# Attention and a mixture of experts in one kernel: weight splits from both ends of the table, norms ahead of the last score products, and sums of squares on TensorE

## The chip, the core and the metric

The kernel is one program on 1 core of a Trainium2 chip. The metric is device time in microseconds (us) of one execution, lower is better. The engines are named as in the profile: PE (TensorE matmul), PEld (TensorE weight load), DVE (VectorE), ACT (ScalarE), POOL (GpSimd) and SP (SyncE, which here only issues DMAs).

## What is computed

Attention over channels for four batches, then a mixture of experts with one expert per token:

```python
# q, k, v: 4 x 5056 x 256 (float32)
qn = q / (norm(q, axis=1) + 1e-06); kn = k / (norm(k, axis=1) + 1e-06)
a = softmax(kn.transpose(0, 2, 1) @ qn / tau)      # 4 x 256 x 256
x = (v @ a).reshape(20224, 256)
e = argmax(x @ w_gate, axis=1); g = softmax(x @ w_gate)[e]
out = g * (relu(x @ w1[e]) @ w2[e])                # 8 experts, 256 -> 1024 -> 256
```

## The kernel before, in words

**Attention** is the generator `attention(b, ...)` (L177). It walks over 20 chunks of 256 tokens of q and k. A chunk (tile `raw`, 128 x 1024 float32) is loaded by two DMAs (L190, L191), squared on ACT (L200, L202) and added into `ssq` on DVE (L203), and multiplied on PE into the score accumulators `sp` in PSUM. Batch 0 and chunks 1 to 13 of batch 1 multiply float32 as it is (L209, two instructions of 128x256 for each product, eight for a chunk). The other chunks are first split into a high and a low float32r part (L173 on ACT, L174 on DVE) and multiplied as such (L213, L214). Batch 1's chunk 0 is split as well, since its 512 wide products open both halves of the accumulators.

After the last chunk come the norms: `ssq` is folded (L220), summed over the partitions by four products with ones (L223, tile `ntp`), a row of 128x4 operations on DVE makes the reciprocal norms (L229 to L242), and the scores become the softmax `a_x` (L263 to L298).

Then ten groups g0 to g9 of 512 tokens follow: load of v (L308), `px` = v times `a_x` on PE (L322), four copies and four sums of squares on ACT (L327, L329), routing on DVE and PE (L335 to L399, with the products `rtp` L380, L383), scaled rows (L343, L344) and four scatters into a table in DRAM on POOL (L402). The loads of chunks and of v take turns in a ring of three tiles (`raw`), and SP issues its DMAs strictly in order.

**Weights** are the generator `weights()` (L92). Sixteen matrices of 1 MB, n = 0 to 15 (w1 and w2 of eight experts), are loaded as float32, each into the place in `W` of the next matrix (`raw = place(n + 1)`, L111; the last one into a tile of its own). PE sums their squares (`gram`, L137, 16 products), DVE takes the diagonal (`w_diag`, L140), PE adds it up (L144) and DVE makes the scales of an expert (`pow2`, L82, L83). Then a matrix is split: ACT writes the high halves and DVE the low ones, into place n.

```python
act.activation(hi, src, AF.Copy, scale=sw)                                   # L105
vec.scalar_tensor_tensor(out=lo, in0=src, scalar=sw, in1=hi, ...)            # L106
```

Split n writes over the raw values of matrix n - 1, so ACT can start split n only when DVE has finished split n - 1: one chain of 16 splits.

**What sets the order.** The program is written as a loop over steps (L658): after batch 0's chunks each step takes half a group of batch 0, two yields of `weights()` (one split) and one chunk of batch 1, ten chunks in all. `table(0)` (L457) comes after group g5 and makes the list of the first expert blocks from the counts so far. A scheduler then fixes the order of the instructions on each engine; each engine works strictly in that order. From the first block on (L548 to L610) expert blocks run to the end, with the rest of the attention in between.

Of the kernel before, what the change touches and what calls it, by code (L numbers as in the profile page):

```python
# [20 lines left out]
P = 128  # L21
B, N, C = 4, 5056, 256
NP = 5120
E, F = 8, 1024
# [6 lines left out]
CUT = 6  # L31
# [30 lines left out]
def attention_then_experts(ctx, tc, q, k, vT, tau, w_gate, w1, w2, kc, out):  # L62
    nc = tc.nc
    sync, act, vec, pool, pe = nc.sync, nc.scalar, nc.vector, nc.gpsimd, nc.tensor

    one = ctx.enter_context(tc.tile_pool(name="one", bufs=1))
    work = ctx.enter_context(tc.tile_pool(name="work", bufs=2))
    tiny = ctx.enter_context(tc.tile_pool(name="tiny", bufs=2))
    dram = ctx.enter_context(tc.tile_pool(name="dram", bufs=1, space=bass.MemoryType.DRAM))
    ps_a = ctx.enter_context(tc.tile_pool(name="ps_a", bufs=2, space=bass.MemoryType.PSUM))  # L70
    ps_h = ctx.enter_context(tc.tile_pool(name="ps_h", bufs=3, space=bass.MemoryType.PSUM))
    ps_y = ctx.enter_context(tc.tile_pool(name="ps_y", bufs=1, space=bass.MemoryType.PSUM))
# [17 lines left out]
    last_load = [None]  # L90

    def weights():  # L92

        def place(n):
            return W[:, n // 2, (n % 2) * 4096 : (n % 2 + 1) * 4096]

        scales = one.tile([P, E, 2], F32, name="scales")
        later = []
        ready = []

        def split_one():
            nonlocal ready
            if ready:
                hi, lo, src, sw = ready.pop(0)
                act.activation(hi, src, AF.Copy, scale=sw)  # L105
                vec.scalar_tensor_tensor(out=lo, in0=src, scalar=sw, in1=hi, op0=ALU.mult, op1=ALU.subtract)  # L106

        for n in range(2 * E):
            e, w = divmod(n, 2)
            if n < 2 * E - 1:  # L110
                raw = place(n + 1).bitcast(F32)  # L111
            else:
                raw = work.tile([P, 2048], F32, tag="hl", name="wraw", bufs=2)
            for h in range(2):
                with tc.issue_after(last_load[0]):
                    if w == 0:
                        sync.dma_start(
                            out=raw.rearrange("p (q d f) -> p q d f", q=4, d=2)[:, :, h, :],
                            in_=w1[e, h * P : (h + 1) * P, :].rearrange("p (q f) -> p q f", q=4),
                        )  # L120
                    else:
                        sync.dma_start(
                            out=raw[:, h * 1024 : (h + 1) * 1024].rearrange("p (f d) -> p f d", d=C),
                            in_=w2[e, h * 512 : (h + 1) * 512, :].rearrange("(f p) d -> p f d", p=P),
                        )
                if h == 0:
                    split_one()
                yield

            top = raw.bitcast(BF16)[:, 1::2]  # L130
            if w == 0:
                gram = ps_h.tile([P, 512], F32, tag="hp", name="gram")
                dsum = tiny.tile([P, 2], F32, name="w_dsum")
            own = gram[:, w * P : (w + 1) * P]
            for i in range(16):
                part = top[:, i * P : (i + 1) * P]
                pe.matmul(own, part, part, start=(i == 0), stop=(i == 15))  # L137
            diag = work.tile([P, P], F32, tag="o", name="w_diag", bufs=2)

            vec.scalar_tensor_tensor(  # L140
                out=diag, in0=own, scalar=1.02, in1=ident, op0=ALU.mult, op1=ALU.mult, accum_out=dsum[:, w : w + 1]
            )
            if w == 1:
                pe.matmul(gram[:, 2 * P : 2 * P + 2], ones, dsum, start=True, stop=True)  # L144
                pow2(scales[:, e, :], gram[:, 2 * P : 2 * P + 2], 10)
            sw = scales[:, e, w : w + 1]

            d4 = place(n).rearrange("p (k s x) -> p k s x", k=8, s=2)
            later.append((d4[:, :, 0, :], d4[:, :, 1, :], raw.rearrange("p (k x) -> p k x", k=8), sw))
            if w == 1:  # L150
                ready, later = ready + later, []
# [12 lines left out]
    NATIVE = 14  # L164
# [9 lines left out]
        vec.tensor_tensor(out=hl[:, 1], in0=raw, in1=hl[:, 0], op=ALU.subtract)  # L174
        return hl

    def attention(b, s_split, x_split, acc):  # L177

# [3 lines left out]
        sp = [pool_.tile([P, 2, C], F32, tag=tag, name=f"sp{c}") for c, (pool_, tag) in enumerate(acc)]  # L182
        ssq = one.tile([P, 2, 512], F32, tag="a_l", name="ssq")
        nch = len(s_split)
        for ch in range(nch):

            tag, bufs = (("raw", RAW), ("rows", 3), ("xg", 2), ("raw", RAW), ("rows", 3))[ch % 5 if b == 0 else 0]
            raw = work.tile([P, 2, 512], F32, tag=tag, name="raw", bufs=bufs)
            sl = slice(2 * ch, 2 * ch + 2)
            sync.dma_start(out=raw[:, :, 0:C], in_=qv[b][:, sl, :])  # L190
            load = sync.dma_start(out=raw[:, :, C:512], in_=kv[b][:, sl, :])  # L191
            if b == 0:
                last_load[0] = load.ins
            if s_split[ch]:
                hl = split(raw)
                sq = raw
            else:
                sq = work.tile([P, 2, 512], F32, tag="hl", name="sq", bufs=2)
            if ch == 0:
                act.activation(ssq, raw, AF.Square)  # L200
            else:
                act.activation(sq, raw, AF.Square)  # L202
                vec.tensor_tensor(out=ssq, in0=ssq, in1=sq, op=ALU.add)  # L203
            for j in range(2):
                first, last = ch == 0 and j == 0, ch == nch - 1 and j == 1
                for c in range(2):
                    kc0 = C + c * P
                    if not s_split[ch]:
                        pe.matmul(  # L209
                            sp[c][:, 0, :], raw[:, j, kc0 : kc0 + P], raw[:, j, 0:C], start=first, stop=last  # L210
                        )
                        continue
                    pe.matmul(sp[c], hl[:, 0, j, kc0 : kc0 + P], hl[:, :, j, 0:C], start=first, stop=False)  # L213
                    pe.matmul(  # L214
                        sp[c][:, 1, :], hl[:, 1, j, kc0 : kc0 + P], hl[:, 0, j, 0:C], start=False, stop=last
                    )
            yield 2 * 640


# [1 line left out]
        tp = ps_t.tile([P, 512], F32, tag="tp", name="ntp")  # L221
        for i in range(4):
            pe.matmul(tp[:, i : i + 1], ssq[:, 0, i * P : (i + 1) * P], ones[:, 0:1], start=True, stop=True)  # L223

        def four(name):
            return tiny.tile([P, 4], F32, name=name)

        ss, y, h = four("n_ss"), four("n_y"), four("n_h")
        vec.tensor_scalar(out=ss, in0=tp[:, 0:4], scalar1=1e-30, scalar2=None, op0=ALU.max)  # L229
# [383 lines left out]
    def run(gen):  # L613
        for _ in gen:
            pass
# [132 lines left out]
```

## Time and profile before

| | |
|---|---|
| runs | 1222.15, 1226.06, 1227.25 us, median 1226.06 |
| the profiled execution | 1222.09 us, span 1220.2 us, mean granted clock 0.988 of 2.4 GHz |
| PE busy | 1161.4 us (95% of the span) |
| DVE, ACT, POOL busy | 904.7 (74%), 645.3 (53%), 383.5 us (31%) |
| PE busy, tenths in the first 8 of 40 slices | 8 8 8 8 7 8 9 8, then 9 nearly throughout |
| DMA busy, the same slices | 9 9 8 9 6 8 5 4 |

A slice is 30.5 us. Busy shares are averages over stages with different limits, so the stages are read one by one below. PE is close to full after the first 150 us; what it leaves free lies ahead of that.

### The profile page before, as it was taken

What the parts mean: (1) busy time and instruction counts of PE and PEld (TensorE: products, weight loads), DVE (VectorE), ACT (ScalarE), POOL (GpSimd) and SP (SyncE); (2) the same over time, 40 slices, a digit from 0 to 9 for tenths busy, and PEclk for the clock granted to TensorE, in tenths of its full rate; (3) what the DMA queues carried; (4) which work ended last, traced back from release to release, by engine and by line L of the source; (5) the groups of instructions that cost most, each with busy time, mean ns of one, the idle gap of its engine ahead of it and who ended that gap; (6) DMA issues with size and microseconds to landing.
All of it is one profiled execution on the core that took longest, in us unless ns stands there. A gap on an engine that the chain in (4) does not pass through costs nothing. (4 is left out here: it accounts for less than half of the span.)

```text
span 1220.2 us, 28272 instructions
## 1 busy us (share of the span) xinstructions
PE 1161.4 (95%) x10212; PEld 1025.4 (84%) x10212; DVE 904.7 (74%) x2384; ACT 645.3 (53%) x1362; POOL 383.5 (31%) x366
## 2 busy tenths in 40 slices
PE   8888789988899999999999999999999999999998
PEld 7767578877788889888888888889888888888897
DVE  5689789677787777777788777777676656656886
ACT  5388864776655545666655545666523332332322
POOL 0027651444521122444441112444431111111111
PEclk9889999999999999999999999999999999999999
DMA  9989685444355433444354534433241222221221
GB/s 302 351 278 316 156 206 136 117 122 131 103 137 127 136 84 96 119 121 109 94 152 114 138 87 96 114 114 79 62 114 48 53 53 53 49 45 42 43 50 33
DMA packets 196830, 145.91 MB, mean 120 GB/s; under 512 B 117580, under 2 KB 176337, under 8 KB 196688
## 3 DMA queue, kind: packets, MB, share of 16 engines
q1 hardware_dynamic: 181296, 102.48, 34.2%
q0 software_dynamic: 15392, 41.60, 9.5%
q8 instruction: 81, 1.33, 0.5%
q14 instruction: 61, 0.50, 0.1%
HBM read 80.03 MB, written 43.29 MB: 101 GB/s over the span
## 5 line engine op out<-in xcount | busy, mean ns | idle before, releaser
L571 PE MATMUL hp<-xT,wp 128*128 128x256 f16 (+1 forms) x4320 | 452.1, 263 | 5.1 <-issue 1.4
L594 PE MATMUL y<-wp,ht 128*128 128x256 f16 x3888 | 450.3, 273 | 6.4 <-DVE ht L579 2.7
L594 PEld LDWEIGHTS <-ht 128*128 128x128 f16 x3888 | 372.4, 98 | 68.1 <-issue 10.4
L571 PEld LDWEIGHTS <-wp 128*128 128x128 f16 x4320 | 383.8, 98 | 52.1 <-issue 6.1
L605 POOL DMA_INDIRECT out<-o,mt x162 | 184.3, 1138 | 649.6 <-ACT o L603 612.4
L559 DVE COPY wp<-W 128x1024 f16 x720 | 297.6, 428 | 111.9 <-PE y L594 64.4
L578 ACT ACTIVATE ht<-hp 128x512 f16<-128x512 f32 x324 | 191.2, 595 | 201.3 <-PE hp L571 162.8
L579 DVE SCALAR_TENSOR_TENSOR ht<-hp,ht 128x512 f16<-128x512 f32 x324 | 220.4, 685 | 36.8 <-ACT ht L578 31.5
L402 POOL DMA_INDIRECT xs<-rows,r_si x160 | 182.3, 1139 | 145.8 <-ACT xjunk L329 50.1
L603 ACT ACTIVATE o<-y,b_fac 128x256 f32<-128x256 f32 x162 | 68.8, 469 | 175.5 <-PE y L594 161.3
L325 PE MATMUL px<-a_h,hl 128*128 128x264 f32 x480 | 99.1, 296 | 1.3 <-ACT xg L327 0.8
L343 ACT ACTIVATE rows<-xg,x_sc 128x256 f16<-128x256 f32 x160 | 69.2, 498 | 35.7 <-issue 16.3
L325 PEld LDWEIGHTS px<-a_h,hl 128*128 128x128 f32 x480 | 79.1, 188 | 4.1 <-issue 1.8
L174 DVE TENSOR_TENSOR hl<-raw,hl 128x1024 fp32r<-128x1024 f32 x47 | 57.4, 1221 | 30.7 <-ACT hl L173 30.7
L213 PE MATMUL sp<-hl 128*128 128x512 f32 x188 | 72.4, 418 | 1.0 <-DVE hl L174 1.0
L173 ACT CAST hl<-raw 128x1024 fp32r<-128x1024 f32 x47 | 49.1, 1044 | 45.0 <-PE sp L214 40.0
L209 PE MATMUL sp<-raw 128*128 128x256 f32 x264 | 64.0, 394 | 9.0 <-DMA raw<-in_k 9.0
L202 ACT ACTIVATE raw<-raw 128x1024 f32<-128x1024 f32 x44 | 46.6, 1058 | 44.6 <-DVE hl L174 42.5
L344 DVE SCALAR_TENSOR_TENSOR rows<-xg,x_sc,rows 128x256 f16<-128x256 f32 x160 | 69.1, 478 | 0.6 <-issue 0.2
L325 PE MATMUL px<-a_l,hl 128*128 128x264 f32 x240 | 68.6, 286 | 0.0
L329 ACT ACTIVATE xjunk<-xg 128x256 bf16<-128x256 f32 x160 | 66.7, 417 | 3.1
L327 ACT COPY xg<-px 128x264 f32<-128x264 f32 x160 | 57.8, 367 | 14.2 <-PE px L325 6.9
(140 smaller groups left out, 925.6 us busy)
## 6 DMA issues: line engine op xcount, KB each, us to landing
raw<-in_q SPq DMA_DIRECT2D x80, 256.0 KB
raw<-in_k SPq DMA_DIRECT2D x80, 256.0 KB
vraw<-in_vT SPq DMA_DIRECT2D x40, 512.0 KB
W<-in_w SPq DMA_DIRECT2D x30, 512.0 KB
out<-o,mt POOLq DMA_INDIRECT x162
xs<-rows,r_si POOLq DMA_INDIRECT x160
xT<-xs SPq DMA_TRANSPOSE x90
xs<-pad SPq DMA_DIRECT2D x9, 129.0 KB
```

The source lines that it names most:

```text
L213: pe.matmul(sp[c], hl[:, 0, j, kc0 : kc0 + P], hl[:, :, j, 0:C], start=first, stop=False)
L325: pe.matmul(px, hl[:, vh, c, ts], ah[:, c, :], start=(n == 0), stop=(n == 5))
L343: act.activation(r16[:, t, 0:C], x, AF.Copy, scale=sc[:, t : t + 1])
L344: vec.scalar_tensor_tensor(out=r16[:, t, C : 2 * C], in0=x, scalar=sc[:, t : t + 1], in1=r16[:, t, 0:C], op0=ALU.mult, op1=ALU.subtract,)
L402: ins = pool.indirect_dma_start(out=xs[:, :], out_offset=bass.IndirectOffsetOnAxis(ap=si[:n, t : t + 1], axis=0), in_=rows[:n, t, :], in_o ...
L559: vec.tensor_copy(out=t, in_=Wf[:, ds(e * 8192 + n * 1024, 1024)])
L571: pe.matmul(hp[:, f % nf, :], wp[:, dc, wh, (f % 2) * P : (f % 2 + 1) * P], xT[:, 2 * xh + dc, :], start=(n == 0), stop=(n == 5),)
L578: act.activation(ht[:, 0], hp, AF.Relu)
L579: vec.scalar_tensor_tensor(out=ht[:, 1], in0=hp, scalar=0.0, in1=ht[:, 0], op0=ALU.max, op1=ALU.subtract)
L594: pe.matmul(ys[j], hts[f // nf][:, hh, f % nf, j * P : (j + 1) * P], wp[:, f % 2, wh, :], start=(f == 0 and n == 0), stop=(f == 7 and n == 2),
L603: act.activation(o, ys[j], AF.Copy, scale=fac[:, j : j + 1])
L605: pool.indirect_dma_start(out=out[:, :], out_offset=bass.IndirectOffsetOnAxis(ap=mt.bitcast(I32)[:, j, 1:2], axis=0), in_=o, in_offset=Non ...
```

## The change

It has four parts. The lines are those of the changed kernel where they carry a +.

1. `weights()` takes the experts from both ends, e = 0, 7, 1, 6, 2, 5, 3, 4. The first kind loads a matrix into the next place as before, the second kind into the place below. The two diagonals of an expert are taken together after both grams.
2. In batch 0 the products of the last two chunks are written behind the norm sums (`behind`).
3. Batch 1's first five chunks get their sums of squares from PE: each of the four 128 wide column blocks is multiplied with itself into a PSUM bank `own`, and four DVE operations (`own_sums`) take the diagonals, written behind batch 0's last group. ACT's squares and DVE's additions for these chunks go.
4. Batch 1's chunk 0 is no longer split; three products with a tile of zeros open `own` and both accumulators instead.

```diff
-        for n in range(2 * E):
-            e, w = divmod(n, 2)
-            if n < 2 * E - 1:
-                raw = place(n + 1).bitcast(F32)
...
+        for i in range(E):
+            up = i % 2 == 0
+            e = i // 2 if up else E - 1 - i // 2
+            pair = (2 * e, 2 * e + 1) if up else (2 * e + 1, 2 * e)
...
+            for k, n in enumerate(pair):
+                if i >= E - 2 and k == 1:
+                    raw = work.tile([P, 2048], F32, tag="hl", name="wraw", bufs=2)
+                else:
+                    raw = place(n + 1 if up else n - 1).bitcast(F32)
+                raws.append(raw)
+                for h in range(2):
+                    load(n, raw, h)
+                    if h == 0:
+                        split_one()
+                    if (k, h) != (1, 1):
+                        yield
...
+            own = list(zip(pair, raws))
+            if len(ready) == 2:
+                own = [ready[0], own[0], ready[1], own[1]]
+                ready.clear()
+            ready.extend(own)
+            yield
...
+            if ch == 0 and by_pe:
+                own.append(ps_y.tile([P, 512], F32, tag="y0", name="own"))
+                none = work.tile([P, 512], F16, tag="o", name="none", bufs=2)
+                vec.memset(none, 0.0)
+                for acc_ in own + [s_.rearrange("p s c -> p (s c)") for s_ in sp]:
+                    pe.matmul(acc_, none[:, 0:P], none, start=True, stop=False)
+            if ch == by_pe:
                 act.activation(ssq, raw, AF.Square)
-            else:
+            elif ch > by_pe:
                 act.activation(sq, raw, AF.Square)
                 vec.tensor_tensor(out=ssq, in0=ssq, in1=sq, op=ALU.add)
...
+                    for i in range(4 if ch < by_pe else 0):
+                        ch_i = raw[:, j, i * P : (i + 1) * P]
+                        pe.matmul(
+                            own[0][:, i * P : (i + 1) * P], ch_i, ch_i, start=False,
+                            stop=ch == by_pe - 1 and j == 1 and i == 3,
+                        )
...
+            if b > 0 or ch < nch - 2:
+                products()
+            else:
+                behind.append(products)
...
-    second = attention(1, [i == 0 or i >= NATIVE for i in range(nch)], True, normal)
+    second = attention(1, [i >= NATIVE for i in range(nch)], True, normal, CUT - 1)
...
     run(first)
+    own_sums()
```

Three places show how the order on the engines moves. The first is DVE between batch 0's softmax (`s_nm`, `s_z`, `a_x`) and the third expert's scales; L106 and L111 are the low half of a split, L140 and L157 the diagonal. Before, and then changed:

```order
L272 TENSOR_REDUCE s_nm<-soft 128x2
L106 SCALAR_TENSOR_TENSOR W<-W,scales 128x8x256
L276 TENSOR_SCALAR s_z<-s_z 128x2
...
L106 SCALAR_TENSOR_TENSOR W<-W,scales 128x8x256
L298 COPY a_x<-gtp 128x2x8
L140 SCALAR_TENSOR_TENSOR w_diag,w_dsum<-gram,kt 128x128 x2
L82 TENSOR_SCALAR pw_m<-gram 128x2
L83 TENSOR_SCALAR scales<-pw_m 128x2
L140 SCALAR_TENSOR_TENSOR w_diag,w_dsum<-gram,kt 128x128
L82 TENSOR_SCALAR pw_m<-gram 128x2
```

```order
L357 COPY a_x<-gtp 128x2x8
L157 SCALAR_TENSOR_TENSOR w_diag,w_dsum<-gram,kt 128x128 x2
L82 TENSOR_SCALAR pw_m<-gram 128x2
L83 TENSOR_SCALAR scales<-pw_m 128x2
L111 SCALAR_TENSOR_TENSOR W<-W,scales 128x8x256 x2
L157 SCALAR_TENSOR_TENSOR w_diag,w_dsum<-gram,kt 128x128 x2
L82 TENSOR_SCALAR pw_m<-gram 128x2
L83 TENSOR_SCALAR scales<-pw_m 128x2
L111 SCALAR_TENSOR_TENSOR W<-W,scales 128x8x256 x2
```

Before, two split halves stand ahead of the third expert's diagonals; now three do, two of them between the second expert's scales and the third's diagonals. On PE the product L144 (now L161) that follows those diagonals stands directly ahead of the first group's `px` in both orders.

The second place is ACT in group g2, whose copies L386 (before: L327) wait for PE; L110 (before: L105) is the high half of a split, L388 the sums of squares of a group, L402 (before: L343) its scaled rows. Before, from g1's rows on, and then changed:

```order
L343 ACTIVATE rows<-xg,x_sc 128x256 x4
L367 ACTIVATE r_d<-r_d 128x32
L327 COPY xg<-px 128x264 x2
L329 ACTIVATE xjunk,x_ss<-xg 128x256
L105 ACTIVATE W<-W,scales 128x8x256
L329 ACTIVATE xjunk,x_ss<-xg 128x256
L327 COPY xg<-px 128x264 x2
L329 ACTIVATE xjunk,x_ss<-xg 128x256
L202 ACTIVATE sq<-raw 128x1024
L329 ACTIVATE xjunk,x_ss<-xg 128x256
L105 ACTIVATE W<-W,scales 128x8x256
```

```order
L402 ACTIVATE rows<-xg,x_sc 128x256 x4
L426 ACTIVATE r_d<-r_d 128x32
L110 ACTIVATE W<-W,scales 128x8x256 x2
L386 COPY xg<-px 128x264
L388 ACTIVATE xjunk,x_ss<-xg 128x256
L386 COPY xg<-px 128x264
L388 ACTIVATE xjunk,x_ss<-xg 128x256
```

The splits, which stood apart with copies between them, now stand in adjacent twos ahead of a group's copies, and the squares are gone here.

The third place is PE between g1's routing product (L442, before: L383) and g2's `px` (L381, before: L322). Before, L144 is the scale product and L209 a chunk:

```order
L209 MATMUL sp_682<-raw 128x256
L144 MATMUL gram<-w_dsum,ones 128x2
L322 MATMUL px<-a_x,vraw 128x264 x4
...
L383 MATMUL rtp<-r_ex,ones_108 128x8
L322 MATMUL px<-a_x,vraw 128x264 x4
```

```order
L442 MATMUL rtp<-r_ex,ones_109 128x8
L161 MATMUL gram<-w_dsum,ones 128x2
...
L237 MATMUL sp_705<-none 128x512
...
L259 MATMUL own<-raw 128x128 x4
...
L259 MATMUL own<-raw 128x128 x4
L249 MATMUL sp_704<-raw 128x256
...
L259 MATMUL own<-raw 128x128 x4
L381 MATMUL px<-a_x,vraw 128x264 x8
```

Between g1's routing and g2's `px` PE now has three opening products and the whole of chunks 0 and 1, with four blocks of `own` products; before, g2's `px` surrounded the routing.

## Rows read from the trace of the kernel before

**Rows 1.** Stretches: PE, PEld, DVE, ACT, POOL busy us (instructions); clock; DMA share; GB/s.

```profile
60.50:86.50 26.00, 20.71 (x130) 16.66 (x131) 20.38 (x44) 21.04 (x40) 5.53 (x4) 0.87 0.84 263
86.50:124.40 37.90, 33.36 (x238) 28.09 (x237) 35.65 (x91) 34.81 (x71) 25.70 (x18) 1.00 0.91 303
124.40:150.00 25.60, 20.28 (x94) 15.24 (x92) 20.33 (x85) 21.01 (x67) 17.62 (x16) 0.93 0.66 176
150.00:1220.20 1070.20, 1036.39 (x9469) 920.76 (x9469) 790.82 (x2095) 538.91 (x1158) 333.77 (x325) 1.00 0.38 97
```

**Rows 2.** Groups of instructions, 42.4 to 150 us: busy us, mean ns, idle before.

```profile
L106 DVE SCALAR_TENSOR_TENSOR W<-W,scales 128x2048 f16<-128x2048 f32 x15 | 35.2, 2349 | 5.5 <-ACT W L105 5.4
...
L105 ACT ACTIVATE W<-W,scales 128x2048 f16<-128x2048 f32 x15 | 30.0, 2000 | 22.4 <-DVE scales L83 14.7 <-DVE W L106 6.5 <-issue 1.2
...
L203 DVE TENSOR_TENSOR ssq<-ssq,sq 128x1024 f32<-128x1024 f32 x9 | 10.9, 1215 | 0.0
L202 ACT ACTIVATE sq<-raw 128x1024 f32<-128x1024 f32 x9 | 9.5, 1053 | 0.0
```

**Rows 3.** Timeline, 60 to 66 us: start, duration, instruction, idle before and its releaser.

```profile
60.11 0.59 PE L144 MATMUL gram<-w_dsum,ones 128*128 128x2 f32 x2 [0.39 <-DVE w_diag L140]
...
60.56 4.54 PE L322 MATMUL px<-a_x,vraw 128*128 128x264 f32 x12
...
61.05 2.35 DVE L106 SCALAR_TENSOR_TENSOR W<-W,scales 128x2048 f16<-128x2048 f32 x1
...
63.48 2.00 ACT L105 ACTIVATE W<-W,scales 128x2048 f16<-128x2048 f32 x1 [3.13 <-DVE W L106]
```

**Rows 4.** Timeline, 36 to 50 us: batch 0's norms and the end of its exponentials.

```profile
36.88 4.91 PE L209 MATMUL sp<-raw 128*128 128x256 f32 x22
...
38.27 0.69 DVE L220 TENSOR_TENSOR ssq<-ssq 128x512 f32<-128x512 f32 x1
...
41.63 0.95 PE L223 MATMUL ntp<-ones,ssq 128*128 128x1 f32 x8
...
42.62 0.16 DVE L229 TENSOR_SCALAR n_ss<-ntp 128x4 f32<-128x4 f32 x1 [3.65 <-PE ntp L223]
...
46.05 0.68 PE L248 MATMUL ntp<-soft,ones 128*128 128x128 f32 x4
...
46.57 0.91 PE L137 MATMUL gram<-W 128*128 128x128 bf16 x13
...
49.83 0.19 ACT L275 ACTIVATION_READ_ACCUMULATOR soft<-soft,s_nm 128x1 f32 x1
```

**Rows 5.** Timeline of PE, 80 to 100 us.

```profile
80.31 0.50 PE L213 MATMUL sp<-hl 128*128 128x512 f32 x1 [0.99 <-DVE hl L174]
...
81.82 1.10 PE L137 MATMUL gram<-W 128*128 128x128 bf16 x16
82.76 1.94 PE L209 MATMUL sp<-raw 128*128 128x256 f32 x8
84.54 0.28 PE L144 MATMUL gram<-w_dsum,ones 128*128 128x2 f32 x2
...
86.54 0.18 PE L380 MATMUL rtp<-r_ex,tri 128*128 128x32 f16 x1
...
95.98 3.81 PE L322 MATMUL px<-a_x,vraw 128*128 128x264 f32 x16
99.63 1.08 PE L137 MATMUL gram<-W 128*128 128x128 bf16 x16
```

**Rows 6.** Timeline of PE: the end of g5's products, and the first expert block.

```profile
123.39 1.05 PE L322 MATMUL px<-a_x,vraw 128*128 128x264 f32 x4
124.28 1.46 PE L209 MATMUL sp<-raw 128*128 128x256 f32 x6
...
149.99 1.48 PE L571 MATMUL hp<-xT,wp 128*128 128x256 f16 x12 [0.97 <-DMA xT<-xs]
```

**Rows 7.** SP's own waits, 30 to 175 us: us in total, times, longest.

```profile
SPq L308 <- PE px L322: 20.6, 5, 9.1
```

More of the change, by code (lines that the diff above doesn't have):

```diff
@@ new lines, in split_one, with load @@
+                n, raw = ready.pop(0)
+                d4 = place(n).rearrange("p (k s x) -> p k s x", k=8, s=2)
+                src, sw = raw.rearrange("p (k x) -> p k x", k=8), scales[:, n // 2, n % 2 : n % 2 + 1]
+                act.activation(d4[:, :, 0, :], src, AF.Copy, scale=sw)
+                vec.scalar_tensor_tensor(
+                    out=d4[:, :, 1, :], in0=src, scalar=sw, in1=d4[:, :, 0, :], op0=ALU.mult, op1=ALU.subtract
+                )
+        def load(n, raw, h):
+            e, w = divmod(n, 2)
+            with tc.issue_after(last_load[0]):
+                if w == 0:
+                    sync.dma_start(
+                        out=raw.rearrange("p (q d f) -> p q d f", q=4, d=2)[:, :, h, :],
+                        in_=w1[e, h * P : (h + 1) * P, :].rearrange("p (q f) -> p q f", q=4),
+                    )
+                else:
+                    sync.dma_start(
+                        out=raw[:, h * 1024 : (h + 1) * 1024].rearrange("p (f d) -> p f d", d=C),
+                        in_=w2[e, h * 512 : (h + 1) * 512, :].rearrange("(f p) d -> p f d", p=P),
+                    )
@@ new lines, in weights @@
+        for i in range(E):
+            up = i % 2 == 0
+            e = i // 2 if up else E - 1 - i // 2
+            pair = (2 * e, 2 * e + 1) if up else (2 * e + 1, 2 * e)
+            gram = ps_h.tile([P, 512], F32, tag="hp", name="gram")
+            dsum = tiny.tile([P, 2], F32, name="w_dsum")
+            raws = []
+            for k, n in enumerate(pair):
[10 more added lines that the diff above has]
+                        yield
+                top = raw.bitcast(BF16)[:, 1::2]
+                own = gram[:, n % 2 * P : (n % 2 + 1) * P]
+                for m in range(16):
+                    part = top[:, m * P : (m + 1) * P]
+                    pe.matmul(own, part, part, start=(m == 0), stop=(m == 15))
+            for w in range(2):
+                diag = work.tile([P, P], F32, tag="o", name="w_diag", bufs=2)
+                vec.scalar_tensor_tensor(
+                    out=diag, in0=gram[:, w * P : (w + 1) * P], scalar=1.02, in1=ident, op0=ALU.mult, op1=ALU.mult,
+                    accum_out=dsum[:, w : w + 1],
+                )
+            pe.matmul(gram[:, 2 * P : 2 * P + 2], ones, dsum, start=True, stop=True)
+            pow2(scales[:, e, :], gram[:, 2 * P : 2 * P + 2], 10)
+            own = list(zip(pair, raws))
[4 more added lines that the diff above has]
+            yield
@@ L175, in split, with own_sums, attention @@
         return hl
-    def attention(b, s_split, x_split, acc):
+    gsum = tiny.tile([P, 4], F32, name="n_gs", bufs=1)
+    own = []
+    def own_sums():
+        for i in range(4):
+            diag = work.tile([P, P], F32, tag="o", name="n_diag", bufs=2)
+            vec.scalar_tensor_tensor(
+                out=diag, in0=own[0][:, i * P : (i + 1) * P], scalar=1.0, in1=ident, op0=ALU.mult, op1=ALU.mult,
+                accum_out=gsum[:, i : i + 1],
+            )
+    def attention(b, s_split, x_split, acc, by_pe=0):
         sp = [pool_.tile([P, 2, C], F32, tag=tag, name=f"sp{c}") for c, (pool_, tag) in enumerate(acc)]
@@ L184, in attention @@
         nch = len(s_split)
+        behind = []
         for ch in range(nch):
@@ L193, in attention @@
                 last_load[0] = load.ins
+            hl = None
             if s_split[ch]:
@@ L200, in attention, with products @@
+            if ch == by_pe:
                 act.activation(ssq, raw, AF.Square)
-            else:
+            elif ch > by_pe:
                 act.activation(sq, raw, AF.Square)
                 vec.tensor_tensor(out=ssq, in0=ssq, in1=sq, op=ALU.add)
[L204 to L208, printed above, removed]
+            def products(ch=ch, raw=raw, hl=hl):
+                for j in range(2):
+                    first, last = ch == 0 and j == 0 and not by_pe, ch == nch - 1 and j == 1
+                    for c in range(2):
+                        kc0 = C + c * P
+                        if not s_split[ch]:
+                            pe.matmul(
+                                sp[c][:, 0, :], raw[:, j, kc0 : kc0 + P], raw[:, j, 0:C], start=first, stop=last
+                            )
+                            continue
+                        pe.matmul(sp[c], hl[:, 0, j, kc0 : kc0 + P], hl[:, :, j, 0:C], start=first, stop=False)
@@ L217, in attention @@
+            if b > 0 or ch < nch - 2:
+                products()
+            else:
+                behind.append(products)
             yield 2 * 640
@@ L223, in attention @@
             pe.matmul(tp[:, i : i + 1], ssq[:, 0, i * P : (i + 1) * P], ones[:, 0:1], start=True, stop=True)
+        for products in behind:
+            products()
         def four(name):
```

60 lines of the change are left out of this document (10 added, 50 removed).

## The prediction

> **What bounds the kernel now.** I read the busy times by stretch first. From 150 us to the end PE is busy 1036.4 of 1070.2 us, 97% [rows 1]: that part lasts as long as its products, and the change leaves them alone, so what it can win or lose lies ahead of it. I cut the time before at three events: the first `px` product at 60.56 [rows 3], g1's routing product at 86.54 [rows 5], the end of g5's products at 124.28 [rows 6]; the first expert block starts at 149.99 and waits for its tokens [rows 6].
>
> In the three stretches between 60.5 and 150 us PE has 5.3, 4.5 and 5.3 us idle, 15.1 in all [rows 1]. Two of them also run partly at the lower of the two clock levels (1.2 against 2.4 GHz): mean clock 0.87 over 26.0 us and 0.93 over 25.6, worth at most 3.4 and 1.8 us. So 20.3 us are to be had. In the middle stretch no engine has much left: DVE 35.7, ACT 34.8, PE 33.4 of 37.9 us [rows 1]. Work that moves from DVE and ACT to PE there moves from two nearly full engines to a third.
>
> The chain of splits shows in the timeline: DVE writes low halves for 2.35 us, then ACT, which had waited 3.13, writes the next high halves for 2.00 [rows 3]; a split takes 4.35 us while each engine works half of it. But ACT's waits for DVE's split sum to only 6.5 us before 150 us, and its 14.7 for scales lie mostly where nothing is queued yet [rows 2].
>
> **The change, part by part.** Durations are from the profiled execution (1222.09 us).
>
> *Sums of squares on PE.* Five chunks get 2 x 4 products of 128x128 float32, 40 in all, 80 instructions, since each float32 product shows as two. The trace has no such stream. Nearest in shape and type is L248: four from 46.05 to 46.57, 0.13 us each [rows 4]. Below it lie the bfloat16 products, sixteen from 81.82 to 82.76, 0.06 each; above it the 256 wide float32 ones, eight from 82.76 to 84.54, 0.22 each [rows 5]. I take 0.13, so 10.4 us, with 4.7 and 17.8 as ends; below nothing is excluded, since products are added. A weight load stands in each of these. The Trainium skill (TensorE: Matmul & The Clock Gate, sections on LDWEIGHTS and on weight-path perf modes) says that float32 weights don't get the fast load and cost columns divided by 1.2 GHz, which for 128 columns is an estimated 107 ns; by that the 80 would cost 8.5 us and the forecast below would be 1.9 us lower. L248's 0.13 is above that figure, and no row before shows the load alone as the pace.
>
> Chunk 0 as float32 takes 1.78 instead of the split chunk's 1.51 (80.31 to 81.82) [rows 5]: 0.3 more. The three opening products are 512 wide; four such and four of half the width made that 1.51, so three cost 0.75. Together PE gets 11.4 us more.
>
> ACT loses one cast and five squares, six times 1.05 = 6.3 us; DVE one subtraction and five additions, six times 1.22 = 7.3 [rows 2]; cast and subtraction are priced by the same shape, and gets four diagonals back, some 1.1.
>
> *Norms first.* The folded sums are ready at 38.96, but L223 starts at 41.63, behind the last chunks' products; DVE waits 3.65 us for it [rows 4]. The order puts four products, one chunk (1.8 us), behind L223. So norms and softmax come 1.8 us earlier: L248 at 44.2, the exponentials' end at 48.2 instead of 50.0 [rows 4].
>
> *Splits.* The branch that would interleave two pairs asks for two splits left over, but both are taken while the next pair loads, so it never runs. Splits come as 0, 1, 15, 14, 2, 3, 13, 12 and so on. Inside a pair ACT still waits for DVE; only between pairs is the chain cut. The first split now follows the exponentials, and third-expert diagonals stand behind three splits on DVE. From 48.2 that is ACT 2.00, DVE 2.35, ACT 2.00, then two halves on DVE, 4.70: 11.05 us, with 0.6 of softmax work between, 59.8. L144 waits for those diagonals and `px` for L144, as before: `px` starts at about 60.5. The 1.8 us are gone again; I count nothing.
>
> *From there to g1's routing.* ACT was busy 21.0 us in this stretch [rows 1]. One split (2.0) moves behind g1's routing, and cast and squares (3.2) go: 15.8, and I add 2.2 for one wait on a DVE half. So the routing comes at 78.5, 8 us earlier.
>
> *From g1's routing to g5's products.* Here the order is against it: chunks 0 and 1, whole, stand ahead of g2's `px`. PE's list: four groups at 3.65 (95.98 to 99.63) = 14.6; six grams at 0.94 = 5.6; five chunks at 1.78 + 16 x 0.13 = 19.3; three plain chunks 5.3; openings 0.75; eight small products at 0.14 (84.54 to the next) 1.1 [rows 5]. That is 46.7 us, ending at 125.2, against 124.3 now. ACT's list is its 34.8 less five squares, plus some two splits, plus three waits of 2.35 inside adjacent pairs, 40.6: covered by PE, with 6 us to spare. If PE is quicker, ACT takes over there.
>
> *Loads.* Each of the 32 weight DMAs is still issued, in another order; no raw place is needed twice before its split. Chunks and v share the ring, and SP waits in order: L308 waited 20.6 us for `px` [rows 7]. Chunk products now hold a tile 2.1 us longer, so the loads behind them come later; by the list above each still lands before PE asks. I count nothing; without that cover it is a rival.
>
> *From g5 to the first block*, 25.7 us [rows 6], the chain of routing, table, scatter and load is the same. PE has two chunks more to do there, 3.6 us, and 5.3 idle [rows 1]: covered.
>
> The sum: 11.4 added, 10.5 of the 20.3 filled, 0.9 us later: 1223.0. The profiled execution lies 0.3% under the median of 1226.06; the four times known (three runs and it) have the mean 1224.4. On that I put the forecast: **1225**, no change. A measurement of this kernel can tell about 0.5%, 6.1 us, from none.
>
> **The rivals.**
> - *The relief is passed on (faster).* DVE and ACT are the fullest engines of the middle stretch and lose 6 us each; if `px` waits for them rather than for PE, and PE's additions fall into its gaps, 17 of 20.3 us are filled and the products cost 0.11: 1224.4 + 9.8 - 17 = 1217. For it: DVE's 94% busy. Against it: g2's `px` stands behind 8 us of chunk work.
> - *The ring is too short (slower).* Place: the three tiles between chunks and v. Five chunks hold theirs 3.9 instead of 1.8 us, SP stands in order behind them, and PE waits 2 us at each of the groups g2 to g5 for v or a chunk: 1225.3 + 8 = 1233. It decides from 1.7 us a group. For it: SP's 20.6 us of such waits. Against it: the loads are issued two items ahead.
> - *The splits stay the bound (no change).* Products at 0.06 shorten PE's list to 41, but ACT's 40.6 with its pair waits holds the groups there: g5 ends 4.7 us earlier, 1220. The interleaving that the code describes isn't in the order.
>
> **How the numbers follow.** Forecast 0.42, passed on 0.28, ring 0.22, splits 0.08. Faster than 0.5% is the second, 0.28; slower the third, 0.22; the other two, 0.50, lie within. All gaps filled would give 1224.4 + 11.4 - 20.3 = 1215.5, none 1235.8; with cheaper products and the scatter of runs the range is 1213 to 1235, which leaves the ends of the dear products out.
>
> **What would show it.** Right: spacing of the `own` instructions near 0.13; L223 starting near 39.9; first `px` near 60.5; g1's routing near 78.5; g5's products ending within 2 us of 125; PE's idle between 60.5 and 150 us down from 15 to under 10. ACT should wait for DVE at the second split of most pairs. Wrong: g5 ending before 120 or after 130, a first block that moves by over 5 us, or a difference that arises after 150 us.

## The result, and the profile after

The changed kernel is slower: median 1232.02 us of six runs (1227.86 to 1233.75) against 1225.9 of six of the kernel before; ratio 1.0060, 95% interval 1.0039 to 1.0081. Taken again in run 18 it was 1.0077 (1.0046 to 1.0108, below). The profiled execution took 1233.75 us, its span is 1231.6. It is the longest of its six, and that of the kernel before (1222.09) as short as the shortest of that kernel's, so the two profiles differ by 11.4 us of span where the medians differ by 6.1.

The busy times by stretch of the changed kernel, cut at its own events (first `px`, g1's routing, ACT's late square, g4's `px`, the end of g5's `px`, first block); columns as in [rows 1]:

```profile
60.71:81.25 20.54, 17.74 (x104) 14.01 (x105) 14.91 (x35) 16.15 (x34) 5.33 (x5) 0.68 0.75 233
81.25:109.97 28.72, 27.88 (x216) 24.82 (x213) 18.64 (x43) 17.85 (x36) 13.33 (x9) 1.00 1.00 321
109.97:119.62 9.65, 6.53 (x36) 5.92 (x37) 6.33 (x23) 6.72 (x11) 0.61 (x2) 0.82 0.32 110
119.62:133.97 14.35, 13.29 (x89) 11.30 (x88) 10.58 (x28) 11.77 (x26) 7.95 (x7) 1.00 0.68 214
133.97:163.95 29.98, 22.52 (x105) 16.93 (x104) 21.63 (x104) 22.29 (x72) 18.43 (x16) 0.92 0.69 179
```

DVE and ACT now have room (18.6 and 17.9 of 28.7 us in the second stretch; before, 35.7 and 34.8 of 37.9 [rows 1]). PE is full there, as forecast, but not in the first, third and last stretch, and the first block starts at 163.95 instead of 149.99 [rows 6].

The timeline of PE in the changed kernel, 60 to 165 us:

```profile
60.26 0.59 PE L161 MATMUL gram<-w_dsum,ones 128*128 128x2 f32 x2 [2.22 <-DVE w_diag L157]
60.71 6.86 PE L381 MATMUL px<-a_x,vraw 128*128 128x264 f32 x16
...
72.53 0.38 PE L161 MATMUL gram<-w_dsum,ones 128*128 128x2 f32 x2 [2.03 <-DVE w_diag L157]
...
81.25 0.18 PE L439 MATMUL rtp<-r_ex,tri 128*128 128x32 f16 x1
...
82.29 0.39 PE L237 MATMUL own<-none 128*128 128x512 f16 x1
82.52 0.59 PE L237 MATMUL sp<-none 128*128 128x512 f16 x2
82.95 1.03 PE L249 MATMUL sp<-raw 128*128 128x256 f32 x4
83.82 1.05 PE L259 MATMUL own<-raw 128*128 128x128 f32 x8
84.71 1.03 PE L249 MATMUL sp<-raw 128*128 128x256 f32 x4
...
89.98 3.73 PE L381 MATMUL px<-a_x,vraw 128*128 128x264 f32 x16
...
108.89 1.08 PE L249 MATMUL sp<-raw 128*128 128x256 f32 x4
113.09 0.38 PE L161 MATMUL gram<-w_dsum,ones 128*128 128x2 f32 x2 [3.12 <-DVE w_diag L157]
...
115.65 1.92 PE L259 MATMUL own<-raw 128*128 128x128 f32 x8
...
130.29 3.72 PE L381 MATMUL px<-a_x,vraw 128*128 128x264 f32 x16
...
162.03 2.13 PE L381 MATMUL px<-a_x,vraw 128*128 128x264 f32 x4 [5.96 <-ACT xg L386]
163.95 1.06 PE L630 MATMUL hp<-xT,wp 128*128 128x256 f16 x4
```

Eight `own` instructions take 0.89 us (83.82 to 84.71), 0.111 each. Three long waits for `w_diag` and one for `xg` stand out; the first of them was 0.39 us before [rows 3]. Behind them PE goes at the lower level, 1.2 GHz, for a while: g0's sixteen `px` take 6.86 us, g2's 3.73; eight `own` take 1.92 at 115.65 and 1.05 at 83.82. The granted clock is 0.68 and 0.82 in these stretches. Part of that is old: g0's first twelve `px` took 4.54 us before [rows 3].

PE's waits between 60 and 165 us (total, times, longest), first of the kernel before:

```profile
PE sp L209 <- DMA raw<-in_k: 4.5, 4, 2.2
PE rtp L380 <- DVE r_ex L363: 3.9, 1, 3.9
PE gram L137 <- ACT xg L327: 3.3, 1, 3.3
PE px L322 <- DMA vraw<-in_vT: 2.9, 1, 2.9
PE px L322 <- ACT xg L327: 2.4, 3, 1.4
PE sp L213 <- DVE hl L174: 1.0, 1, 1.0
PE hp L571 <- DMA xT<-xs: 1.0, 1, 1.0
PE gram L144 <- DVE w_diag L140: 0.4, 1, 0.4
```

and of the changed kernel, all there are:

```profile
PE gram L161 <- DVE w_diag L157: 9.3, 6, 3.1
PE px L381 <- ACT xg L386: 7.4, 4, 6.0
PE px L381 <- ACT xjunk L388: 0.6, 1, 0.6
```

The waits for loads are gone in this execution (run 18 has one of 1.4 us for v). Those for `w_diag` and for `xg` at `px`, small before, have grown to 9.3 and 7.4 us. The sum is much the same: 17.3 us against 19.4, and in the second pair (runs 18 and 17) 19.1 against 17.6.

Two of the long ones, followed back. DVE in the changed kernel ahead of the first `px`: two low halves in a row, then the diagonals.

```profile
55.17 4.61 DVE L111 SCALAR_TENSOR_TENSOR W<-W,scales 128x2048 f16<-128x2048 f32 x2
59.70 0.28 DVE L157 SCALAR_TENSOR_TENSOR w_diag<-gram,kt 128x128 f32<-128x128 f32 x1
```

The 3.12 us at 113.09 begin on ACT. The square of chunk 5, the first that ACT still makes, stands ahead of g3's last copy, and its chunk is not there yet:

```profile
110.09 1.06 ACT L239 ACTIVATE ssq<-raw 128x1024 f32<-128x1024 f32 x1 [2.81 <-DMA raw<-in_q]
111.05 0.36 ACT L386 COPY xg<-px 128x264 f32<-128x264 f32 x1
```

On DVE the row maximum of g3 (`r_m`) waits for that copy until 111.44, and the diagonals for L161 stand behind it. SP had waited for `own` products to release ring tiles before it could issue chunk loads (two of its waits, 60 to 150 us; behind the gap, the issue of chunk 5's first load):

```profile
SPq L222 <- PE rtp L442: 14.0, 2, 9.9
SPq L222 <- PE own L259: 7.5, 2, 5.4
...
103.68 0.37 SPq L222 DMA_DIRECT2D raw<-in_q  x1
```

The first row names a routing product, which reads no ring tile; `own` products end just ahead of both of its issues, at 99.92 and 117.57. For chunk 5 the wait is 2.1 us, and from issue to the square are another 6.4, in a stretch in which the DMA engines are busy all the time (share 1.00). How much of the delay is the ring's and how much the traffic's no run here separates.

The last long wait: DVE has `b_fac` of the first block in its row, which needs `mt`; g8's routing stands behind it, ACT behind that, and the `px` at 162.03 behind ACT. In the kernel before (second and third line) DVE waits for `mt` in the same way, and PE behind it, but only after the first block has begun. So part of this wait was there before, at another place.

```profile
160.60 0.23 DVE L645 TENSOR_SCALAR b_fac<-mt,fe 128x2 f32<-128x2 f32 x1 [6.10 <-DMA mt<-xs]
...
151.04 0.23 DVE L586 TENSOR_SCALAR b_fac<-mt,fe 128x2 f32<-128x2 f32 x1 [3.67 <-DMA mt<-xs]
...
155.77 0.19 PE L380 MATMUL rtp<-r_ex,tri 128*128 128x32 f16 x1 [3.86 <-DVE r_ex L363]
```

### The profile page after: what moved, and what is told of

Its sections match the earlier page's. It is cut to its first block, busy times and chain, and to the rows that moved or that the text cites. A ratio compares the mean times of both kernels' runs of the same rounds, so it can differ in the third digit from the quotient of the medians.

```text
span 1231.6 us, 28431 instructions
## 1 busy us (share of the span) xinstructions
PE 1175.5 (95%) x10295; PEld 1038.7 (84%) x10295; DVE 900.6 (73%) x2387; ACT 641.9 (52%) x1356; POOL 376.4 (31%) x366
## 4 chain that ended last, share of the span: by engine, by line
PE 57%; issue 25%; DVE 7%; POOL 5%; ACT 3%; DMA 2%; POOLq 0%; another core or an unknown queue 0%; SPq 0%; DVEq 0%; ACTq 0%
PE hp L630 20%; PE y L653 18%; PE px L384 7%; POOL out L664 4%; PE sp L249 4%; PE sp L253 3%; PE sp L254 2%; PE px L381 1%; DVE ht L638 1%; DVE hl L192 1%; ACT W L110 1%; DVE W L111 1%; DMA raw<-in_k 1%; DVE rows L403 1%; DVE wp L618 1%
## 5 line engine op out<-in xcount | busy, mean ns | idle before, releaser
L402 ACT ACTIVATE rows<-xg,x_sc 128x256 f16<-128x256 f32 x160 | 69.1, 498 | 33.7 <-DVE r_ex L435 13.9
L192 DVE TENSOR_TENSOR hl<-raw,hl 128x1024 fp32r<-128x1024 f32 x46 | 56.1, 1220 | 29.3 <-ACT hl L191 29.3
L403 DVE SCALAR_TENSOR_TENSOR rows<-xg,x_sc,rows 128x256 f16<-128x256 f32 x160 | 69.6, 477 | 0.3 <-issue 0.3
L388 ACT ACTIVATE xjunk<-xg 128x256 bf16<-128x256 f32 x160 | 66.6, 416 | 3.5
L386 ACT COPY xg<-px 128x264 f32<-128x264 f32 x160 | 58.0, 366 | 16.3 <-PE px L384 9.6
```

The source lines that it names most:

```text
L402: act.activation(r16[:, t, 0:C], x, AF.Copy, scale=sc[:, t : t + 1])
L403: vec.scalar_tensor_tensor(out=r16[:, t, C : 2 * C], in0=x, scalar=sc[:, t : t + 1], in1=r16[:, t, 0:C], op0=ALU.mult, op1=ALU.subtract,)
```

## The experiments

Ratios are to the kernel before on the same chip, with 95% intervals; the chips differ (before takes 1231 us on the chips of runs 1 to 8 and 13 to 18, 1193 on that of 9 to 12), so spans of different jobs are compared only with care. Every run is a program of its own, for which the order on the engines is fixed anew, so a part that is taken out takes its place in the order with it. Theory A at the start: PE's added products make the loss. Theory B: the order of the splits. Theories C and D are told where they come up.

**Run 1, squares alone.** Parts 3 and 4 on the kernel before (`weights()` of before, all products ahead of the norms).

> The kernel before with parts 3 and 4 alone (squares of batch 1's first five chunks by PE, zero products that open the accumulators); weights and norms as before. Theory A, the price of the products: in the changed kernel's trace a block of 8 own instructions takes 0.89 us, so 80 take 8.9, with openings and chunk 0 some 10 us on PE; if they alone make the loss and DVE's and ACT's relief is worth little, this run is slower than before by more than the whole change: ratio 1.006 to 1.009, and g5's products end over 5 us later than 124.3. Theory B, the order of the splits makes the loss: this run lies within 0.997 to 1.003, and g5's products end within 3 us of 124.3.

Measured 1.0070 (1.0043 to 1.0097); g5's `px` end at 129.4. As A has it.

**Run 2, splits alone.** Part 1 on the kernel before; the edit is shown against the changed kernel, whose line numbers the run keeps.

```diff
-            if b > 0 or ch < nch - 2:
+            if True:
                 products()
...
-    second = attention(1, [i >= NATIVE for i in range(nch)], True, normal, CUT - 1)
+    second = attention(1, [i == 0 or i >= NATIVE for i in range(nch)], True, normal)
...
-    own_sums()
```

> The kernel before with part 1 alone (experts from both ends, two diagonals taken together). Theory A: nothing of the loss is here, ratio 0.995 to 1.001. Theory B: low halves stand ahead of the diagonals on DVE and PE waits for them, as at 60.3, 72.5 and 113.1 us of the changed kernel (2.2, 2.0 and 3.1 us idle, and the granted clock falls to 0.75 in that stretch): ratio 1.003 to 1.007, with PE's waits for w_diag summing to over 6 us ahead of the first block.

Measured 1.0048 (1.0028 to 1.0068). As B has it in size, but the waits for `w_diag` are only 3.6 us between 60 and 165, where B asked for over 6; the largest is another:

```profile
PE sp L249 <- DMA raw<-in_k: 7.0, 3, 3.8
PE px L381 <- ACT xg L386: 4.5, 4, 2.2
PE gram L161 <- DVE w_diag L157: 3.6, 2, 2.9
PE gram L153 <- DMA wraw<-in_w: 2.0, 3, 0.9
```

**Run 3, norms alone.** `behind` with all else as before.

> The kernel before with part 2 alone (products of the last two chunks behind the norm sums). Both theories: norms 1.8 to 2.1 us earlier, the third expert's diagonals and the first px about as before, ratio 0.997 to 1.001. If the first px starts 1.5 us or more ahead of 60.56, the norms do set it, and the ratio is 0.997 to 0.999.

Measured 0.9989 (0.9963 to 1.0016), first `px` at 60.55: nothing, as forecast.

**Run 4, the change without the squares.**

> The changed kernel without parts 3 and 4 (squares on ACT and DVE for every chunk of batch 1, chunk 0 split as before). Theory A: the loss goes with the products, ratio to before 0.995 to 1.000. Theory B: the loss stays, 1.003 to 1.007.

Measured 1.0036 (1.0012 to 1.0059), as B has it. So both parts cost alone, and they don't add up to the whole.

**Run 5, no own products:** the whole change without them.

```diff
-                    for i in range(4 if ch < by_pe else 0):
+                    for i in range(0):
```

> The changed kernel without the 80 own instructions on PE; the sums of squares of batch 1's first five chunks are left out of the norms altogether, all else stays (opening products, diagonals, order of splits, norms). Theory A, the products take a place on a PE that has none free: their 8.9 us come back, ratio to before 0.997 to 1.000. Theory C, the loss is waits (diagonals behind low halves, late chunks) and PE had gaps for the products: ratio 1.003 or more.

Measured 1.0003 (0.9976 to 1.0029), just above A's range. The loss goes when the products go. What is left, the relief of ACT and DVE together with the new splits and the norms, comes to nothing; beside run 4 (1.0036), which has the same splits and norms without the relief, the relief may be worth some 0.3%, within the intervals.

The products' time isn't all that went. The order changed too: chunk 5's square now stands behind g3's rows and a split on ACT, and its chunk is there.

```profile
106.15 1.71 ACT L402 ACTIVATE rows<-xg,x_sc 128x256 f16<-128x256 f32 x4 [2.10 <-issue]
107.76 1.99 ACT L110 ACTIVATE W<-W,scales 128x2048 f16<-128x2048 f32 x1
109.66 1.04 ACT L239 ACTIVATE ssq<-raw 128x1024 f32<-128x1024 f32 x1
```

So this run doesn't tell the products' price from the order that came with them, and no other run holds the order fixed.

**Run 6, squares and norms, splits of before.**

> The changed kernel with the splits of before (parts 2, 3 and 4 alone). The squares alone gave 1.0070, the splits alone 1.0048, the whole 1.0060, so the parts don't add up. If the splits cost as much beside the squares as alone, this run is near 1.001 to 1.002; if the two losses are the same waits or the splits fill what the squares lose, it is 1.005 to 1.008.

Measured 1.0046 (1.0024 to 1.0068): between the two ranges, near the whole change, with the old splits.

**Run 7, one spare tile,** on the splits alone. New in the splits is also a second tile `wraw`, in the ring `hl` that holds the squares (theory D). The last expert's pair is taken upward, so that one such tile is enough, as before.

```diff
-            pair = (2 * e, 2 * e + 1) if up else (2 * e + 1, 2 * e)
+            pair = (2 * e, 2 * e + 1) if up or i == E - 1 else (2 * e + 1, 2 * e)
...
-                if i >= E - 2 and k == 1:
+                if i == E - 1 and k == 1:
...
-                    raw = place(n + 1 if up else n - 1).bitcast(F32)
+                    raw = place(n + 1 if up or i == E - 1 else n - 1).bitcast(F32)
```

> The run with the splits alone (1.0048), but the last expert's pair is taken upward, so that only its second matrix needs a tile outside W, as before; the order of the splits is the same up to the last pairs. Theory D, the second tile wraw takes one of the two hl tiles that the squares' results need, from 94 us on, and holds up ACT, the chunk ring and so the loads: ratio 0.998 to 1.001, and PE's waits for chunk loads ahead of 150 us fall from 7.0 to under 3 us. Theory B, the order of low halves and diagonals: ratio stays at 1.003 to 1.006.

Measured 1.0058 (1.0038 to 1.0078). PE's waits for chunks fell (7.0 to 1.4 us from 42 to 165) and the time did not: D falls, and once more waits only changed places.

**Run 8, diagonals apart** (each taken right after its own gram), on the splits alone, and **run 16**, the same beside **run 15**, the splits alone again.

```diff
-                    if (k, h) != (1, 1):
+                    if h == 0:
                         yield
...
                     pe.matmul(own, part, part, start=(m == 0), stop=(m == 15))
+                diag = work.tile([P, P], F32, tag="o", name="w_diag", bufs=2)
+                vec.scalar_tensor_tensor(out=diag, in0=own, ...)
+                if k == 0:
+                    yield
-            for w in range(2):
...
```

> The run with the splits alone (1.0048), but each diagonal is taken right after its own gram and ahead of the next split, as before. Theory B: PE's waits for w_diag (4.9 us there) fall below 3 and the ratio to 0.999 to 1.002. Theory D: no difference to the splits alone, 1.003 to 1.006.

> The run with the splits alone (1.0048) beside the next one on one chip. If the splits cost by themselves: 1.003 to 1.006; if that chip's scatter made it: 0.998 to 1.002.

> The splits alone with each diagonal right after its own gram (1.0020). If diagonals behind low halves make the splits' loss, it lies 0.2 to 0.5% under the run beside it, at 0.999 to 1.002; if not, the two agree within 0.15%.

Measured 1.0020 (0.9993 to 1.0048) in run 8; side by side 1.0060 (1.0041 to 1.0079) for run 15 and 1.0025 (1.0001 to 1.0048) for run 16. The splits cost some 0.5%, and the diagonals in one place seem to be over half of it; the last two intervals just overlap. PE's waits for `w_diag` fell (run 15: 3.6; run 16: 0.8 and 0.7), but those for `px` rose:

```profile
PE px L381 <- ACT xg L386: 6.9, 4, 2.9
PE gram L153 <- DMA wraw<-in_w: 5.0, 2, 3.0
```

**Run 9, relief alone.** Run 6 without the own products.

> The run with squares and norms (1.0046) without the 80 own instructions; the sums of squares of batch 1's first five chunks are left out of the norms. What is left of the change is the relief of ACT and DVE, with the splits of before. Theory A: the products' price goes, 1.0046 less 0.0057 to 0.0073 (what their removal gave from the whole change, and all of their 8.9 us), so 0.997 to 0.999, and the relief is worth at most 0.3%. If the relief of 13 us on ACT and DVE were worth what the prediction took (10 us of PE's idle time filled), this run would be 0.990 to 0.994.

Measured 0.9985 (0.9975 to 0.9995), with run 12 the narrowest interval: 1.8 us for taking some 13 us off ACT and DVE together, with only the opening products left of the price. The order on ACT differs from run 6's here too.

**Run 10, the whole change with diagonals apart.**

> The whole change, but each diagonal is taken right after its own gram and ahead of the next split, as before. If diagonals behind two low halves cost the whole change time too (PE's waits for w_diag there 10.8 us between 42 and 165 us), ratio 1.002 to 1.005 and those waits under 6 us. If PE's added products are all that counts, 1.005 to 1.008 whatever the waits do.

Measured 1.0084 (1.0065 to 1.0103): no better, though PE's waits for `w_diag` between 42 and 165 us fell from 10.8 to 4.5. The first `px` came at 63.13.

**Run 11, real alternation.**

```diff
-            if len(ready) == 2:
-                own = [ready[0], own[0], ready[1], own[1]]
-                ready.clear()
-            ready.extend(own)
+            if up:
+                held = own
+            else:
+                ready.extend([held[0], own[0], held[1], own[1]])
```

> The whole change, but the splits of two experts do alternate (0, 15, 1, 14, 2, 13, ...): a pair from the lower end is held until its partner's scales are there. If ACT's wait for DVE's half inside a pair (5.0 us between 60 and 150 us in the changed kernel) is what holds the groups, this run is 1.001 to 1.004 and that wait is under 2 us. If it isn't on the path, as the prediction took it, 1.004 to 1.008.

Measured 1.0044 (1.0028 to 1.0060): on the edge between the two; no clear gain over the whole change. The wait that was to go didn't go. ACT's waits for DVE's low half between 60 and 150 us, in the changed kernel and in run 11:

```profile
ACT W L110 <- DVE W L111: 5.0, 2, 2.5
...
ACT W L110 <- DVE W L111: 7.8, 4, 2.6
```

So the run can't say what that wait is worth.

**Run 12, splits mended, no squares on PE** (runs 4, 8 and 11 together).

> The change without squares on PE (1.0036), with real alternation and each diagonal right after its gram: the splits as they were meant, norms first. If the order of diagonals was the whole loss of the splits, 0.997 to 1.001; if two chains also give time, under 0.997; if the splits from both ends cost in another way (loads, the second spare tile, low halves ahead of routing), 1.002 to 1.005.

Measured 1.0020 (1.0010 to 1.0030). Two real chains with early diagonals still cost a little. No version here that does all the work is faster than the kernel before beyond the noise (run 3, the nearest, has 0.9989).

**Runs 13 and 14, dose,** on the whole change. Two chunks instead of five (`normal, 2`); every product twice:

```diff
+                        pe.matmul(own[0][:, i * P : (i + 1) * P], ch_i, ch_i, start=False, stop=False)
                         pe.matmul(
```

> The whole change with the squares of two chunks instead of five by PE: 32 own instructions instead of 80, 48 x 0.111 = 5.3 us less on PE, three squares and additions back on ACT and DVE. Theory A, the loss is the price of the products: 1.0060 less 0.0043, so 1.001 to 1.003. If the loss comes with the order of splits and loads: 1.004 to 1.007.

> The whole change with every own product written twice, 160 instructions instead of 80 (the sums of these five chunks count double in the norms). Theory A: another 8.9 us land whole, 0.7% more than the whole change, ratio 1.011 to 1.015. If PE had gaps for such products: 1.005 to 1.009.

Measured 1.0104 (1.0078 to 1.0130) with 32 instructions, above both ranges, and 1.0074 (1.0048 to 1.0101) with 160, in the range that stands for gaps on PE. Theory A falls in its plain form: the loss is not the number of products times their price. With every product twice PE's waits between 60 and 165 us shrink instead, to 11.6 us from the whole change's 17.3 and 19.1:

```profile
PE gram L161 <- DVE w_diag L157: 7.2, 6, 2.3
PE px L382 <- issue: 2.0, 1, 2.0
PE rtp L440 <- DVE r_ex L423: 0.7, 1, 0.7
...
112.45 1.06 ACT L239 ACTIVATE ssq<-raw 128x1024 f32<-128x1024 f32 x1 [0.49 <-DMA raw<-in_k]
```

The last line shows one place: PE reaches g3's `px` 4.7 us later (108.17), and chunk 5's square, still ahead of g3's last copy, waits 0.49 us for its chunk instead of 2.81. Here products did fill a gap.

**Runs 17 and 18, before and the whole change on one chip.**

> The kernel before, profiled beside the next run. If the idle time behind 165 us belongs to the chip: ratio 1.000 within 0.2%, and PE idle there over 33 us on a chip where the kernel before takes 1230 us or more, 29 where it takes 1226, about 10 where it takes 1193. If it belongs to the changed orders, 29 or less here on any chip but the fastest.

> The whole change once more. By the ledger of PE's time (work at the full clock, time lost to the lower clock, idle time) the first pair gave +6.5, +7.6 and -2.7 us. If the products' price is the lasting part, the work term is +6 to +11 us again and the ratio 1.004 to 1.008; if the lower clock made the loss and came by chance, the clock's term is within 2 us of before's and the ratio under 1.004.

Measured 1.0006 (0.9985 to 1.0027) for the kernel before against itself, and 1.0077 (1.0046 to 1.0108). PE's idle time behind 165 us was 33.3 us in run 17, by which most of what the other runs on such chips show there (31.8 to 42.1) goes with the chip; it is 9.7 to 11.1 in runs 9 to 12.

**The ledger.** For each profiled execution the span is split into PE's idle time, the time lost to the lower clock (busy time times one less the granted clock, added up over stretches of 5 us), and the rest, the work at the full clock. Some of PE's records can be missing from a trace, and one execution differs from the next, so a term is good to some us.

| kernel | span | work | clock | idle | of clock and idle: ahead of 165 us | behind |
|---|---|---|---|---|---|---|
| before, first and run 17 | 1220.2, 1226.3 | 1149.8, 1149.2 | 11.6, 16.5 | 58.8, 60.6 | 39.2, 39.5 | 31.2, 37.6 |
| whole change, first and run 18 | 1231.6, 1236.1 | 1157.4, 1159.7 | 18.1, 14.9 | 56.1, 61.5 | 38.7, 35.9 | 35.6, 40.5 |
| run 5, no own products | 1229.1 | 1152.5 | 12.1 | 64.5 | 37.4 | 39.2 |
| run 6, squares and norms | 1232.5 | 1162.4 | 11.0 | 59.1 | 31.5 | 38.6 |
| run 15, splits alone | 1237.4 | 1153.3 | 14.5 | 69.6 | 41.7 | 42.4 |
| run 13, two chunks | 1243.6 | 1156.4 | 19.3 | 67.9 | 39.1 | 48.0 |
| run 14, products twice | 1241.7 | 1170.7 | 12.7 | 58.3 | 28.2 | 42.7 |

Against before the whole change has 7.6 and 10.5 us more work, and got back 0.5 and 3.6 ahead of 165 us where the forecast had 10.5; 4.4 and 2.9 are lost behind. The lower clock is no lasting part of the loss: it took 6.5 us more in the first pair and 1.6 less in the second. The work term is less sharp than it looks: run 15, which gives PE the same products as before, has 3.5 to 4.1 us more of it. And with 31.2 and 37.6 us of idle and slow time behind 165 us, the kernel before leaves nearly as much of PE free there as ahead of it, not only ahead of 150 us as its profile was read at the start.

## Why the prediction was wrong

The range, 1213 to 1235, held the median; the forecast "no change" did not hold. Two of the prediction's own signs of being wrong came: g5's products ended behind 130 (133.97; 131.1 in run 18), and the first block moved by 14 us. One of its signs of being right came too and meant little: PE's idle time between 60.5 and 150 us fell from 15.1 to 9.2 us (11.3 in run 18), but the 5.96 us at 162 lie behind that window.

1. **Products: right, a little dear.** 0.111 us for the 0.13 taken: 8.9 instead of 10.4. With openings of 0.66 (0.75) and 0.2 for chunk 0 (0.3) PE got 9.8 us for the 11.4 forecast; the ledger's 7.6 and 10.5 lie around it. The Trainium skill (TensorE: Matmul & The Clock Gate, LDWEIGHTS), whose figure gave an estimated 107 ns, was nearer than the row of L248. Taking it would have moved the forecast further from the result.
2. **Norms: right.** L275 (then L223) started at 39.58 (39.9), the first `px` at 60.71 (60.5), and run 3 shows no gain.
3. **To g1's routing: the time right in one execution, in part by luck.** 81.25 in the first, 78.50 in run 18, for 78.5. The working went by ACT's list with 2.2 us for one wait on a DVE half; PE's own waits there were for DVE's diagonals (2.03 and, in run 18, 2.27 us) and for `xg` (0.77 and 1.70).
4. **From there to g5: wrong.** 52.7 us instead of 46.7 (81.25 to 133.97), 52.6 in run 18 (78.5 to 131.1). The list went as written until 108.89; then came the chain of chunk 5: late load, ACT's square, g3's copy, DVE's diagonals, L161. It was said of loads that "by the list above each still lands before PE asks". PE didn't ask first: ACT did, for a square ahead of a copy, and the list of ACT held no wait for loads. Of the 6 us too many, that chain is 3.1 and a second wait for `w_diag` (127.59) 1.1; the slower products at 113 to 119 us, where the granted clock is 0.82, are some 1.2 by their busy time.
5. **g5 to the first block: wrong.** 30.0 us for 25.7 (30.4 in run 18). DVE in its order waited 6.10 us for `mt` with routing behind it, and PE's own order put a `px` behind that routing ahead of the first block's products.
6. **The step that failed is the sum's second term,** "10.5 of the 20.3 filled". The 10.5 was read from no wait: it is the 11.4 added less the 0.9 by which the two lists (items 3 and 4) let g5 end later. In its place the ledger shows 0.5 and 3.6 us got back ahead of 165 us. The prediction took idle time of PE as room that relief of ACT and DVE, or more products, would fill. Run 9 puts the relief with the old splits at 1.8 us. The waits that were followed back above hung on what stands ahead in the order of ACT and DVE, not on how much these have to do. DVE's 94% busy in the middle stretch was no sign of a bound that PE was waiting for. Room there was all the same: in run 14 another 8.9 us of products cost next to nothing, so it depends on the order whether a gap is filled.
7. **Splits: "I count nothing" was wrong.** Alone they cost 0.48 and 0.60%. That the alternating branch never runs was right, and ACT waits for DVE inside pairs (2.47 us at 89.54); alternating in earnest (run 11) brought little, but didn't take that wait away either.

Of the rivals, the ring came out at the measured time, 1233, but with its place mostly wrong: no wait of PE for `v` or a chunk is left in the first execution (1.4 us for `v` in run 18), and the ring showed once, through ACT, with 3.1 us and the slow products behind it instead of 2 us at each of four groups. The relief passed on is refuted by the result, and by run 9, where the relief alone gives 1.8 us of the 17 it counted on. The third rival, the splits as the bound, had g5's products end 4.7 us earlier than before; they ended 9.7 us later.

What stays open: why two chunks cost more than five (run 13). Its ledger has 48.0 us behind 165 us, the most of all, which its change does not touch. Two programs that differ in one part can thus differ by some 0.3% in a way that these runs don't explain, and no single ratio under that should be read as the price of a part. With the first 80 products goes a loss of some 0.6% (whole change against run 5, run 6 against run 9); the second 80 cost less than 0.5% by the intervals and about nothing by the medians. That the added work of the first 80 is the cause is supported by runs 5, 6 and 9 and the ledger. The rival, that it is the order which comes with the products, is not excluded: leaving the products out changed the order, doubling them cost nothing, and fewer of them cost more.

## What to carry over

Idle time of a nearly full engine is room only if one knows what each wait in it is for. Here its waits hung on the order of other engines, so that lighter ACT and DVE gave almost nothing with the old splits, and a new order made other waits of about the same sum. Before work is moved to the fullest engine, run the kernel with that work left out altogether: run 9 puts the gain without the products at 0.15% for the order that came of it, too little to pay for 8.9 us of products.

## What was not expected of the hardware

The same kernel before takes 1193 us on one chip and 1231 on others. It was not profiled on the faster one, but the four variants that were show where most of the difference lies: PE idles 9.7 to 11.1 us after 165 us in them, and 30.0 to 42.1 in all other profiles. That is 19 to 32 of the 38 us; the rest, and the reason, stay open.
